# Merged weight words kept in SBUF, and a reordered passage from block 0 to block 1, in a convolution followed by an MLP

## The chip, the cores and the metric

One core of a Trainium2 chip runs the whole program. The metric is device time in microseconds (us), the median of several runs. One further execution was profiled; every row shown here comes from it. Engines: PE is TensorE, DVE VectorE, ACT ScalarE, POOL GpSimd, SP the queue that issues the DMAs.

## The reference

A convolution over the last 7 tokens whose weights differ by token and by head come out of a softmax, and then a two-layer MLP on 16384 tokens of width 192 with 2048 hidden units:

```python
w = softmax(weight_gen)                       # 7 taps, 8 heads
h_in = einsum('bshk,bskhg->bshg', w, windows_of(x_pad))
h = h_in.reshape(16384, 192) @ w_in           # 192 -> 2048
g = where(h >= 1, h, where(h <= -1, 0, (h + 1) ** 2 / 4))
out = g @ w_out                               # 2048 -> 192
```

## The kernel before

The 16384 tokens are 32 blocks of 512. For each block POOL makes the convolution (`conv`: seven products and six additions of 128x768 elements, L179 and L189). The result is turned (a transpose on DVE and a trip through DRAM from block 2 on, on PE for blocks 0 and 1) and split into a high part `hc` (ACT, L258) and a rest `hl` (L259; on DVE for blocks 0 and 1, on POOL from block 2 on).

The MLP runs over pairs: pair w is two slices of 128 hidden units; a block has NP = 8 pairs, so pair 8 is the first of block 1 and pair 16 the first of block 2. The first product of a pair, `gemm1_pair` (18 pairs of matmuls, L378), writes two of the four banks `ps_h` of PSUM. Then follow `relu` and `square` on ACT (L389, L392), `act_g` on DVE (L397), and `split_g`, which makes `gh` on ACT (L403) and `gl` on DVE (L404) and lets the pair's banks go. The second product, `gemm2_part` in two parts (L432), comes two pairs later on PE (LAGP = 2) and adds into the banks `o0` and `o1`; `evac` copies these out when a block is done. A matmul that takes a bank over to the other half of the rows waits for a note that passes over SP (L441).

During block 0 the weights are still being decoded, one chunk c for each pair: a cast (`cast_dve` L331, `cast_act` L327), then `merge` (L340, DVE) joins two halves of each word, `high` (L352, ACT) rounds the word to `whi` or `wo`, and `low` (L356, DVE) keeps the rest in `wlo` or `wo`. `merge` reads two tiles in SBUF (`r` and `head`) and writes `psw`, a tile from the four banks `ps_h`; `low` reads `psw` from PSUM and `whi` or `wo` from SBUF. `early_pair(w)` is the order of this work for pairs 2 to 6, with chunk w + 1; `first_pairs` is the same for the first chunks, `edge_pair` for pair 7, in which block 1 is turned (`turn1`) and split. The convolution of block 1 runs on POOL meanwhile; each of its steps waits for the last `merge` or cast ahead of it (`marks`, a dependency by hand).

All engines run in the order in which the code issues (a manual schedule). What belongs to later blocks is put into that order by a table, `at(w, place)`: the softmax of a group of two blocks (L149 to L155), the convolution, the turning and the splitting. For the group of blocks 3 and 4 (b == 3 in the table) the last softmax step, a multiplication, is POOL's; it stands between the convolutions of blocks 2 and 3 in POOL's order. The splitting of block 2 stands on POOL behind the first six steps of block 3's convolution.

Of the kernel before, what the change touches and what calls it, by code (L numbers as in the profile page):

```python
# [10 lines left out]
F32 = mybir.dt.float32  # L11
# [11 lines left out]
def kernel(  # L23
# [22 lines left out]
    P = 128  # L46
# [53 lines left out]
    def run(ops):  # L100
        for o in ops:
            o()
# [227 lines left out]
        o, i = tops(c, part)  # L330
        marks.append(nc.vector.tensor_scalar(out=o, in0=i, scalar1=0.5, scalar2=None, op0=ALU.mult))  # L331

    psw = {}

    def merge(c, part):
        word = raw_t[c].bitcast(U32)[:, 1:1 + 2 * CN].rearrange("p (c t) -> p c t", t=2)[:, :, 0]
        upper = heads[c % 2].rearrange("p c t -> p (c t)").bitcast(U32)
        psw[c, part] = ps_h.tile([P, 512], F32, tag="h", name="psw")
        sl = (slice(0, C1), slice(C1, CN))[part]
        marks.append(nc.vector.scalar_tensor_tensor(  # L340
            out=psw[c, part].bitcast(U32)[:, 0:sl.stop - sl.start], in0=word[:, sl], scalar=13, in1=upper[:, sl],
            op0=ALU.logical_shift_right, op1=ALU.bitwise_or))
# [48 lines left out]
    def square(i):  # L391
        nc.scalar.activation(out=u_t[i], in_=u_t[i], func=AF.Square, scale=UNIT ** -0.5)  # L392

    def act_g(i):

        uv, pv = u_t.pop(i), h_t[i][:, 0:N]
        nc.vector.scalar_tensor_tensor(out=pv, in0=uv, scalar=1.0 / UNIT, in1=pv, op0=ALU.min, op1=ALU.max)  # L397

    def split_g(i):
        gv = h_t.pop(i)[:, 0:N]  # L400
        gh = gp.tile([P, 512], F32R, tag="gh", name="gh")
        gl = gp.tile([P, 512], F32R, tag="gl", name="gl")
        nc.scalar.activation(out=gh[:, 0:N], in_=gv, func=AF.Copy)  # L403
        nc.vector.tensor_tensor(out=gl[:, 0:N], in0=gv, in1=gh[:, 0:N].bitcast(F32), op=ALU.subtract)  # L404
        g_t[i] = (gh, gl)
# [74 lines left out]
    def at(w, *ops, place=2):  # L480
        side.setdefault((w, place), []).extend(ops)
# [15 lines left out]
    for b in range(2, NB):  # L497
        w = (b - 2) * NP
        at(max(w - 5, 2), lambda b=b: clear_x(b))
        at({2: 4, 3: 8, 4: 14}.get(b, w - 3), lambda b=b: load_x(b), place=4 if b == 4 else 2)  # L500
        if b in first and b > 2:
            g = first[b]
            at({3: 5, 5: 12}.get(b, w - 9), lambda g=g: load_w(g))
            if b == 3:
                where = [(7, 4), (7, 4), (8, 4), (8, 4), (10, 4), (10, 4), (11, 2)]
            elif b == 5:
                where = [(18, 4), (19, 4), (20, 0), (20, 4), (21, 4), (22, 4), (23, 4)]
            else:
                where = [(w - 6 + k, 4) for k in range(7)]
            later(lambda g=g, b=b: softmax(g, nc.vector, nc.gpsimd if b == 3 else nc.vector), where)  # L510
        if b == 2:
            where = [(6, 2)] * 2 + [(7 + k // 3, 2) for k in range(2 * K - 3)]
        elif b == 3:
            where = [(v, 2) for v in (12, 12, 13, 13, 13, 13, 14, 14, 15, 15, 16, 16, 17)]
        elif b == 4:
            where = [(17 + k // 2, 2) for k in range(2 * K - 1)]
        else:
            where = [(w + CONV + k // 2, 2) for k in range(2 * K - 1)]
        later(lambda b=b: conv(b, nc.gpsimd), where)
        turned = [(w + TOUT, 2), (w + TOUT + 1, 0)] + [(w + TOUT + 2 + c, 0) for c in range(NC) for h in range(2)]  # L520
        where = [(w + SPLIT + k // 4, (0, 0, 4, 4)[k % 4]) for k in range(2 * NC)]
        if b == 2:
            turned = [(11, 0)] * 2 + [(12, 0)] * 2 + [(13, 0)] * 2 + [(14, 0)] * 2
            where = [(13, 4)] * 2 + [(14, 4)] * 2 + [(15, 0)] * 2
        elif b == 3:
            turned = [(w + 11, 0)] * 2 + [(w + 12, 0)] * 3 + [(w + 13, 0)] * 3
            where = [(w + 13, 4)] * 2 + [(w + 14, 0)] * 4
        elif b == 4:
            turned[0] = (w + TOUT, 4)
        later(lambda b=b: transpose_out(b), turned)  # L530
        later(lambda b=b: split_out(b, [nc.gpsimd] * NC), where)

    with tc.manual_schedule():
# [51 lines left out]
        def turn1(c):  # L585
            src1.append(ps_h.tile([P, 512], F32, tag="h", name="psx"))
            turn_sum(src1, turned1, True, True, c)
# [68 lines left out]
        def edge_pair(w):  # L656
            i, j = 2 * w, 2 * w + 1
            splits = split_x(1, src1, [nc.vector] * NC)
            relu(i)
            square(i)  # L660
            run(splits[0:1])
            act_g(i)
            run(splits[1:2])
            run(splits[2:3])
            run(splits[3:4])
            turn1(2)
            split_g(i)
            relu(j)
            run(splits[4:6])
            square(j)  # L670
            act_g(j)
            split_g(j)

        at(NP - 2, lambda: again(turned1), place=4)
        at(NP - 1, lambda: turn1(0), lambda: turn1(1), place=5)
        for w in range(NS // 2 + LAGP):
            i, j = 2 * w, 2 * w + 1
            copies, store = [], None
            if i < NS and w != 1:
                gemm1_pair(w)  # L680
            run(side.pop((w, 5), []))
            if w >= LAGP:
                gemm2_part(w - LAGP, 0)
                if w == NP - 1:
                    edge_pair(w)
                gemm2_part(w - LAGP, 1)
                pb, pf = steps[j - 2 * LAGP]
                if pf == NF - 1:
                    copies, store = evac(pb)
                    if i < NS:  # L690
                        at(w + (5 if pb else 6), store, place=0)
            if w < NP:
                run(side.pop((w, 0), []))
                if w == 0:
                    first_pairs()
                elif 1 < w < NP - 1:
                    early_pair(w)
                run(side.pop((w, 2), []))
            else:
                if i < NS:  # L700
                    relu(i)
                    square(i)
                run(side.pop((w, 0), []))
                if i < NS:
                    relu(j)
                if i < NS:
                    square(j)
                    act_g(i)
                    act_g(j)
                if i < NS:  # L710
                    run(copies)
                else:
                    for m in range(n // 2 if store else 0):
                        run(copies[2 * m:2 * m + 2])
                        store(m)
                run(side.pop((w, 2), []))
                if i < NS:
                    split_g(i)
                    split_g(j)
            run(side.pop((w, 4), []))  # L720
# [31 lines left out]
```

## Time and profile before

| | us |
|---|---|
| median of 3 runs | 1144.56 (1143.82 to 1144.73) |
| profiled execution | 1144.88 |
| its span, first to last instruction | 1142.4 |
| PE busy | 1128.4 (99%) |
| ACT busy | 964.5 (84%) |
| DVE busy | 834.3 (73%) |
| POOL busy | 792.4 (69%) |

The span is cut short by 2.5 us against the execution's own time. The shares are means over stages that differ: nearly all of PE's idle time lies in the first 60 us, so the stages have to be read one by one.

### The profile page before, as it was taken

How to read it: one execution, taken by the hardware profiler on the slowest of the kernel's cores; microseconds unless marked ns; L12 is line 12 of the kernel's file. 1: busy time of each engine (PE TensorE's matmuls, PEld its weight loads, DVE VectorE, ACT ScalarE, POOL GpSimd, SP SyncE). 2: the span in 40 equal slices, each digit the busy share in tenths (PEclk: the TensorE clock that was granted, in tenths of full speed). 3: DMA queues.
4: the chain of work that ended last, by engine and by line, in shares of the span. 5: the costliest groups of instructions: out<-in, count | busy, mean ns of one | idle time of the engine just before them, and what ended most of it. 6: DMA issues, size and time to landing. Idle time of an engine off the chain costs nothing.

```text
span 1142.4 us, 32241 instructions
## 1 busy us (share of the span) xinstructions
PE 1128.4 (99%) x12885; PEld 1112.8 (97%) x12885; DVE 834.3 (73%) x1271; ACT 964.5 (84%) x1745; POOL 792.4 (69%) x511
## 2 busy tenths in 40 slices
PE   7999999999999999999999999999999999999998
PEld 5889999999999999999999999999999999999998
DVE  8887867777676777767777677776767777677765
ACT  6878888888888888888888888888888888888886
POOL 4699876777857678486686866778576785866310
PEclk9899999999999999999999999999999999999999
DMA  9512222222222122222122222222222122221100
GB/s 230 116 67 83 92 85 92 72 64 79 90 78 91 59 74 89 73 96 90 44 90 73 86 91 78 65 73 90 77 92 72 61 91 82 81 91 43 48 24 29
DMA packets 84053, 91.43 MB, mean 80 GB/s; under 512 B 5056, under 2 KB 75712, under 8 KB 83904
## 3 DMA queue, kind: packets, MB, share of 16 engines
q1 hardware_dynamic: 83904, 89.39, 24.6%
q8 instruction: 101, 1.65, 0.6%
q14 instruction: 48, 0.39, 0.1%
HBM read 64.99 MB, written 24.38 MB: 78 GB/s over the span
## 4 chain that ended last, share of the span: by engine, by line
PE 96%; ACT 1%; DVE 1%; DMA 0%; POOL 0%; issue 0%; SPq 0%; DVEq 0%; POOLq 0%
PE psh L378 49%; PE o L432 46%; PE psx L267 1%; DMA x<-in_x_dram 0%; ACT u L392 0%; ACT u L389 0%; ACT gh L403 0%; DVE psh L397 0%; DVE psw L340 0%; ACT whi L352 0%; POOL piece L189 0%; POOL acc L189 0%; ACT wo L352 0%; DVE gl L404 0%; DVE wo L356 0%
## 5 line engine op out<-in xcount | busy, mean ns | idle before, releaser
L432 PE MATMUL o<-wo,gh 64*128 64x384 f32 x4096 | 638.3, 353 | 1.0 <-SPq L441 1.0
L432 PE MATMUL o<-wo,gl 64*128 64x192 f32 x4096 | 615.1, 247 | 0.0
L432 PEld LDWEIGHTS o<-wo,gh 64*128 64x128 f32 x4096 | 609.3, 184 | 2.4 <-SPq L441 1.2
L432 PEld LDWEIGHTS o<-wo,gl 64*128 64x128 f32 x4096 | 591.3, 188 | 0.7
L397 DVE SCALAR_TENSOR_TENSOR psh<-u,psh 128x512 f32<-128x512 f32 x512 | 354.4, 695 | 282.2 <-ACT u L392 281.8
L378 PE MATMUL psh<-hc,whi 64*128 64x512 f32 x1536 | 436.6, 396 | 3.6 <-DVE wlo L356 2.5
L378 PE MATMUL psh<-hc,wlo 64*128 64x512 f32 x1536 | 430.5, 389 | 0.0
L378 PE MATMUL psh<-hl,whi 64*128 64x512 f32 x1536 | 429.5, 388 | 0.0
L389 ACT ACTIVATE u<-psh 128x512 f32<-128x512 f32 x512 | 301.4, 589 | 79.0 <-PE psh L378 77.8
L404 DVE TENSOR_TENSOR gl<-psh,gh 128x512 fp32r<-128x512 f32 x512 | 345.2, 684 | 15.5 <-ACT gh L403 1.1
L403 ACT ACTIVATE gh<-psh 128x512 fp32r<-128x512 f32 x512 | 299.0, 591 | 64.7 <-DVE psh L397 64.7
L189 POOL TENSOR_TENSOR acc<-acc,pr 128x768 f32<-128x768 f32 x185 | 343.4, 1856 | 6.5 <-DVE head L331 2.8
L392 ACT ACTIVATE u<-u 128x512 f32<-128x512 f32 x512 | 324.3, 633 | 16.0
L179 POOL TENSOR_TENSOR pr<-x,w 128x768 f32<-128x768 f32 x186 | 286.6, 1548 | 7.0 <-DVE psw L340 7.0
L378 PEld LDWEIGHTS psh<-hc,whi 64*128 64x128 f32 x1536 | 270.6, 185 | 8.7 <-DVE wlo L356 3.9
L378 PEld LDWEIGHTS psh<-hl,whi 64*128 64x128 f32 x1536 | 270.5, 185 | 3.1 <-DVE hl L259 0.3
L378 PEld LDWEIGHTS psh<-hc,wlo 64*128 64x128 f32 x1536 | 270.9, 186 | 1.6
L259 POOL TENSOR_TENSOR hl<-XT,hc 128x512 fp32r<-128x512 f32 x90 | 115.8, 1303 | 206.9 <-PE o L432 151.6
L179 POOL TENSOR_TENSOR acc<-x,w 128x768 f32<-128x768 f32 x31 | 47.9, 1546 | 70.2 <-DVE w L155 68.3
L258 ACT ACTIVATE hc<-XT 128x512 fp32r<-128x512 f32 x90 | 55.5, 618 | 0.0
L284 DVE STREAM_TRANSPOSE T<-acc 128x768 f32<-128x768 f32 x30 | 50.2, 1672 | 0.0
L457 DVE SCALAR_TENSOR_TENSOR osb<-o,osb 128x384 f32<-128x384 f32 x64 | 32.5, 548 | 2.8 <-ACT osb L456 2.8
(44 smaller groups left out, 188.8 us busy)
## 6 DMA issues: line engine op xcount, KB each, us to landing
x<-in_x_dram SPq DMA_DIRECT2D x28, 960.0 KB, 5.0
XT<-D SPq DMA_DIRECT2D x180, 128.0 KB, 2.7
out_dram<-osb SPq DMA_DIRECT2D x31, 384.0 KB, 3.1
D<-T SPq DMA_DIRECT2D x30, 384.0 KB, 2.3
x<-in_x_dram SPq DMA_DIRECT2D x4, 945.0 KB
w<-in_weight_gen_dram SPq DMA_DIRECT2D x15, 224.0 KB, 2.6
r<-in_moe_w_in_dram SPq DMA_DIRECT2D x16, 192.0 KB, 7.3
r<-in_moe_w_out_dram SPq DMA_DIRECT2D x8, 384.0 KB, 12.5
```

Source lines behind the costliest of these rows:

```text
L179: held(eng.tensor_tensor(out=t, in0=xtile[:, k:k + n, :].rearrange("p j (h g) -> p j h g", h=H), in1=wt[:, gi, :, :, k:k + 1].to_broadcast ...
L189: held(eng.tensor_tensor(out=o, in0=s, in1=t, op=ALU.add))
L258: ops.append(lambda c=c: nc.scalar.activation(out=hc[:, c], in_=src[c], func=AF.Copy))
L259: ops.append(lambda c=c: lows.append(engines[c].tensor_tensor(out=hl[:, c], in0=src[c], in1=hc[:, c].bitcast(F32), op=ALU.subtract)))
L284: lambda: nc.vector.transpose(out=T.rearrange("p b c j -> p b j c"), in_=acc.rearrange("p j (r b) -> p b j r", b=R)),
L378: nc.tensor.matmul(out=pair[h][:, 0:N], lhsT=l[rows, f // 2, (c + h) % NC if b < 2 else c], rhs=r[rows, c], start=(s == 0), stop=(s == len ...
L389: nc.scalar.activation(out=u_t[i], in_=h_t[i][:, 0:N], func=AF.Relu, scale=0.5 * UNIT, bias=0.5)
L392: nc.scalar.activation(out=u_t[i], in_=u_t[i], func=AF.Square, scale=UNIT ** -0.5)
L397: nc.vector.scalar_tensor_tensor(out=pv, in0=uv, scalar=1.0 / UNIT, in1=pv, op0=ALU.min, op1=ALU.max)
L403: nc.scalar.activation(out=gh[:, 0:N], in_=gv, func=AF.Copy)
L404: nc.vector.tensor_tensor(out=gl[:, 0:N], in0=gv, in1=gh[:, 0:N].bitcast(F32), op=ALU.subtract)
L432: mm = nc.tensor.matmul(out=o_t[b][turn][:, k, 0:cols], lhsT=g_t[i][l][rows, t * P:(t + 1) * P], rhs=wo[rows, f].rearrange("p s d -> p (s ...
```

## The change

Three edits, and one table row. First, `merge` writes a tile `words` in SBUF, of which one is made for the whole run, with four slots (two chunks, two parts), in the one buffer that the turned blocks (`XT`) use later. The four `ps_h` banks are left to the first product and to block 1's turning. Second, the second product of pair 6 is issued within `edge_pair(7)`, in front of block 1's first product, and the first two turns of block 1 come after the first part of pair 5's second product. Third, the copies of block 0's result come before the squares of pair 9, and the third split of block 1 comes after a square. The softmax table of the group of blocks 3 and 4 moves by one to two pairs.

```diff
-    psw = {}
+    psw, words = {}, []
...
-        psw[c, part] = ps_h.tile([P, 512], F32, tag="h", name="psw")
+        if not words:
+            words.append(xt.tile([P, 4, C1], F32, tag="XT", name="words", bufs=1))
+        psw[c, part] = words[0][:, 2 * part + c % 2]
...
             if b == 3:
-                where = [(7, 4), (7, 4), (8, 4), (8, 4), (10, 4), (10, 4), (11, 2)]
+                where = [(9, 4), (9, 4), (10, 0), (10, 4), (11, 4), (11, 4), (12, 0)]
...
             run(splits[2:3])
             run(splits[3:4])
+            gemm2_part(w - LAGP, 1)
+            gemm2_part(w - 1, 0)
             turn1(2)
+            gemm2_part(w - 1, 1)
             split_g(i)
             relu(j)
-            run(splits[4:6])
             square(j)
             act_g(j)
+            run(splits[4:6])
             split_g(j)
 
         at(NP - 2, lambda: again(turned1), place=4)
-        at(NP - 1, lambda: turn1(0), lambda: turn1(1), place=5)
...
-            run(side.pop((w, 5), []))
             if w >= LAGP:
-                gemm2_part(w - LAGP, 0)
+                if w != NP:
+                    gemm2_part(w - LAGP, 0)
                 if w == NP - 1:
+                    turn1(0)
+                    turn1(1)
                     edge_pair(w)
-                gemm2_part(w - LAGP, 1)
+                elif w != NP:
+                    gemm2_part(w - LAGP, 1)
...
                     relu(i)
+                    if w == NP + 1:
+                        run(copies)
+                        copies = []
                     square(i)
```

DVE in an early pair of block 0, from the merges of one chunk on. Before:

```order
L340 SCALAR_TENSOR_TENSOR psw<-r,head 128x384 x2
L356 TENSOR_TENSOR wlo<-psw,whi 128x384
L356 TENSOR_TENSOR wo<-psw,wo 128x2x192
L397 SCALAR_TENSOR_TENSOR psh<-u,psh 128x512
L331 TENSOR_SCALAR head<-r 128x384
```

And after:

```order
L342 SCALAR_TENSOR_TENSOR words<-r,head 128x384 x2
L358 TENSOR_TENSOR wlo<-words,whi 128x384
L358 TENSOR_TENSOR wo<-words,wo 128x2x192
L399 SCALAR_TENSOR_TENSOR psh<-u,psh 128x512
L331 TENSOR_SCALAR head<-r 128x384
```

The order is the same; the word that `low` reads is now a tile in SBUF, as `whi` and `wo` are.

DVE in pairs 10 and 11 (block 1): the ends of the softmax of blocks 3 and 4 (`s`) and the transpose of block 2 (`T`). Before:

```order
L397 SCALAR_TENSOR_TENSOR psh<-u,psh 128x512 x2
L404 TENSOR_TENSOR gl<-psh,gh 128x512 x2
L153 TENSOR_SCALAR s<-s 128x64
L154 RECIPROCAL s<-s 128x64
L284 STREAM_TRANSPOSE T<-acc 128x6x4x32
L397 SCALAR_TENSOR_TENSOR psh<-u,psh 128x512 x2
L404 TENSOR_TENSOR gl<-psh,gh 128x512 x2
```

And after:

```order
L399 SCALAR_TENSOR_TENSOR psh<-u,psh 128x512 x2
L406 TENSOR_TENSOR gl<-psh,gh 128x512 x2
L152 TENSOR_REDUCE s<-w 128x64
L284 STREAM_TRANSPOSE T<-acc 128x6x4x32
L399 SCALAR_TENSOR_TENSOR psh<-u,psh 128x512 x2
L406 TENSOR_TENSOR gl<-psh,gh 128x512 x2
L153 TENSOR_SCALAR s<-s 128x64
L154 RECIPROCAL s<-s 128x64
```

The reciprocal, for which POOL's multiplication waits, has moved behind pair 11's work and behind the transpose. POOL's own order is the same in both kernels.

PE from the third turn of block 1 to the products that follow it (a second product is 16 such rows of L432, of which the last or first stand here). Before:

```order
L267 MATMUL psx<-ident,piece 128x128 x4
...
L432 MATMUL o_408<-wo,gl 128x192 x2
L378 MATMUL psh<-hc,whi 128x512 x2
...
L378 MATMUL psh<-hl,whi 128x512 x2
L432 MATMUL o_407<-wo,gh 128x384 x2
```

And after:

```order
L267 MATMUL psx<-ident,piece 128x128 x4
...
L434 MATMUL o_403<-wo,gl 128x192 x2
L380 MATMUL psh<-hc,whi 128x512 x2
...
L380 MATMUL psh<-hl,whi 128x512 x2
L380 MATMUL psh<-hc,whi 128x512 x2
```

Before, pair 6's second product stood between the first products of pairs 8 and 9; now these two follow each other.

## Rows read from the trace of the kernel before

**Rows 1.** Windows: busy PE, PEld, DVE, ACT, POOL (us), granted clock, DMA.

```profile
30.00:40.00 10.00, 9.84 (x72) 8.69 (x74) 8.77 (x18) 7.97 (x16) 6.31 (x4) 0.67 0.92 182
60.00:80.00 20.00, 20.00 (x230) 18.18 (x230) 16.66 (x25) 14.67 (x27) 19.07 (x12) 1.00 0.16 52
```

**Rows 2.** Timeline of DVE, one early pair: start, duration, line, operation.

```profile
44.89 1.02 DVE L340 SCALAR_TENSOR_TENSOR psw<-r,head 128x384 uint32<-128x384 uint32 x2
46.01 0.56 DVE L356 TENSOR_TENSOR wlo<-psw,whi 128x384 fp32r<-128x384 f32 x1
46.48 0.55 DVE L356 TENSOR_TENSOR wo<-psw,wo 128x384 fp32r<-128x384 f32 x1
...
50.11 1.02 DVE L340 SCALAR_TENSOR_TENSOR psw<-r,head 128x384 uint32<-128x384 uint32 x2
```

**Rows 3.** Timeline of POOL: block 1's convolution in block 0.

```profile
19.11 0.98 POOL L155 TENSOR_TENSOR w<-w,s 128x448 f32<-128x448 f32 x1 [7.11 <-DVE psw L340]
21.92 1.54 POOL L179 TENSOR_TENSOR acc<-x,w 128x768 f32<-128x768 f32 x1 [1.83 <-DVE psw L340]
23.42 3.05 POOL L179 TENSOR_TENSOR pr<-x,w 128x768 f32<-128x768 f32 x2
...
46.06 1.55 POOL L179 TENSOR_TENSOR pr<-x,w 128x768 f32<-128x768 f32 x1 [1.33 <-DVE psw L340]
...
53.19 1.85 POOL L189 TENSOR_TENSOR piece<-acc,pr 128x768 f32<-128x768 f32 x1
```

**Rows 4.** Timeline, POOL: a product during block 1.

```profile
114.20 1.56 POOL L179 TENSOR_TENSOR pr<-x,w 128x768 f32<-128x768 f32 x1
```

**Rows 5.** Timeline, DVE: one subtraction twice, both inputs in SBUF.

```profile
114.56 1.68 DVE L150 TENSOR_TENSOR w<-w,m 128x448 f32<-128x448 f32 x1
...
183.48 0.61 DVE L150 TENSOR_TENSOR w<-w,m 128x448 f32<-128x448 f32 x1
```

**Rows 6.** Groups by line and shape: count, busy us, mean ns.

```profile
L356 DVE TENSOR_TENSOR wlo<-psw,whi 128x384 fp32r<-128x384 f32 x8 | 4.4, 547 | 1.4 <-ACT whi L352 1.2
```

**Rows 7.** The same view for ACT, split from SBUF and from PSUM.

```profile
L258 ACT ACTIVATE hc<-XT 128x512 fp32r<-128x512 f32 x90 | 55.5, 618 | 0.0
...
L258 ACT ACTIVATE hc<-psx 128x512 fp32r<-128x512 f32 x6 | 3.2, 594 | 0.4 <-PE psx L267 0.3
```

**Rows 8.** Timeline of DVE, first chunks.

```profile
19.55 1.02 DVE L356 TENSOR_TENSOR wo<-psw,wo 128x384 fp32r<-128x384 f32 x2
...
22.30 0.54 DVE L356 TENSOR_TENSOR wlo<-psw,whi 128x384 fp32r<-128x384 f32 x1
...
28.42 1.03 DVE L340 SCALAR_TENSOR_TENSOR psw<-r,head 128x384 uint32<-128x384 uint32 x2
```

**Rows 9.** Timeline of PE: where pair 8's first product begins.

```profile
59.82 0.42 PE L378 MATMUL psh<-hc,whi 64*128 64x512 f32 x2
```

**Rows 10.** The chain that ended last: one second product, start and us.

```profile
62.05 2.25 PE o L432 x32
```

**Rows 11.** Timeline of DVE, pairs 10 and 11.

```profile
73.79 1.45 DVE L404 TENSOR_TENSOR gl<-psh,gh 128x512 fp32r<-128x512 f32 x2
75.16 1.80 DVE L153 TENSOR_SCALAR s<-s 128x64 f32<-128x64 f32 x1
...
77.46 1.61 DVE L284 STREAM_TRANSPOSE T<-acc 128x768 f32<-128x768 f32 x1
...
80.33 1.29 DVE L404 TENSOR_TENSOR gl<-psh,gh 128x512 fp32r<-128x512 f32 x2
```

**Rows 12.** Timeline of PE: first product of pair 13; then, pair 16's end.

```profile
81.45 0.72 PE L378 MATMUL psh<-hc,whi 64*128 64x512 f32 x2
...
96.37 0.39 PE L378 MATMUL psh<-hl,whi 64*128 64x512 f32 x1
```

**Rows 13.** Timeline of POOL: softmax's multiplication, splits of block 2.

```profile
77.68 0.98 POOL L155 TENSOR_TENSOR w<-w,s 128x448 f32<-128x448 f32 x1 [0.78 <-ACT u L392]
...
93.36 2.71 POOL L259 TENSOR_TENSOR hl<-XT,hc 128x512 fp32r<-128x512 f32 x2
```

## Prediction

> **What bounds the kernel now.** I read the windows first. From 60 us on PE has no idle time [rows 1], so work taken off another engine there gives nothing, and a stop that the change puts into PE's row there costs its whole length. Block 0, before that, is another matter. I read it on DVE's timeline: the merges of one chunk begin at 44.89 and those of the next at 50.11, 5.22 us apart [rows 2], while PE needs 2 x 2.25 at most for a pair (a second product is 2.25 [rows 10], a first product no more). So in block 0 DVE paces the pairs, and PE waits for it. [...] The third thing to see is how POOL and DVE meet. At 114.56 a DVE subtraction with both inputs in SBUF takes 1.68 us where the same one takes 0.61 at 183.48, with POOL idle [rows 5]. POOL's product of that time ends at 114.20 + 1.56 = 115.76 [rows 4]; the subtraction ends at 116.24, so it began to run at 115.63, about 0.13 before the product's recorded end. It waited for nearly the whole of POOL's instruction. `low` at 46.48 takes 0.55 in the midst of POOL's product of 46.06 [rows 2, 3]: with the word in PSUM it has one input in SBUF, and does not wait.
>
> **Words in SBUF.** `low` gets two inputs in SBUF (16 times); `merge` had them already, and POOL's steps wait for it by hand. The instructions themselves do not change in price: `low` takes 547 ns for 384 elements from PSUM [rows 6], the subtraction 0.61 for 448 from SBUF [rows 5], about the same per element. [...] ACT's `high` reads SBUF too: 618 against 594 ns for a split [rows 7], 16 x 0.02 = 0.4 us, taken as nothing because ACT waits for DVE in these pairs; without that cover it is 0.4.
>
> The wait is the cost. In an early pair POOL's product starts 1.17 us after the first merge, and the first `low` 1.12 after it [rows 2, 3]. Whichever is first, one `low` waits for a product: if POOL, the first `low`; if DVE, POOL waits half a microsecond and then holds off the second. That is 1.55 - 0.13 = 1.42 on DVE. It swallows the waits for ACT that DVE has now, such as the 0.1 between 44.89 + 1.02 and 46.01 [rows 2], which I put at 0.2 for a pair: 5.22 becomes 6.4. If the second `low` could run on ahead of a waiting POOL, that case would cost nothing; no row shows two such DVE instructions in a row against POOL, so the bounds are 0 and 1.42. I take 1.42, since the row at 114.56 shows that who waits gets the port at the next instruction's end. [...]
>
> From the merges of chunk 3 (28.42 [rows 8]) to those of chunk 7 (50.11) four periods took 21.7; they become 4 x 6.4 = 25.6: +3.9. Ahead of them lie the first chunks. The pair of `low` at 19.55 [rows 8] waits for POOL's softmax step of 19.11 (0.98 [rows 3]), which now starts behind the `low` in front of it: about 0.75. The `low` at 22.30 comes some 0.4 behind the start of POOL's first product (21.92): 1.55 - 0.13 - 0.4 = 1.0. The next meets POOL's second product, queued right behind (23.42): 1.42. Together 3.2. So chunk 7's merges come 7.1 late. POOL's last two additions wait for these merges and then for one `low` (0.5): the convolution of block 1, which ended at 53.19 + 1.85 = 55.04 [rows 3], ends 7.6 late.
>
> **Pair 6's second product.** Pair 8's first product started at 59.82 [rows 9], 4.8 after that end. Now 2.25 of pair 6 stand in front of it, and the first part of pair 5's second product (1.1) runs while PE waits for POOL. So it starts at 59.82 + 7.6 + 2.25 - 1.1 = 68.6. Of this 2.25 is work taken from behind, so the end moves by 68.6 - 59.82 - 2.25 = **+6.5**.
>
> The move has a price behind it. Pairs 8 and 9 now follow each other on PE, so from there PE stands 2.25 nearer to ACT and DVE than before. The first product of pair w + 2 takes the banks that `gl` of pair w lets go. Pair 10's `gl` ended at 73.79 + 1.45 = 75.24 and pair 11's at 80.33 + 1.29 = 81.62 [rows 11]; pair 13's first product began at 81.45 [rows 12], with no slack; pair 12's, one period earlier ((81.45 - 59.82) / 5 = 4.33), at 77.12, with 1.9. Less 2.25 these are -2.2 and -0.4. For pair 11 the table gives back some: between the two `gl` stood `s`, reciprocal and transpose (75.16 to about 79); now only a reduction, taken like the subtraction's 0.61, and the transpose, 1.61, stand there: about 1.6 less. For pair 10 it takes: the maximum and the subtraction (0.6 each) now come right ahead of it, and the subtraction meets POOL, busy 19.07 of 20 us [rows 1]: up to 1.4 more. That the copies come sooner only shifts 1 us from one pair to the next. The stops add up to between 1 and 2.5; I take **+2.0**, nearer the upper end because POOL is almost never idle there.
>
> **Softmax later.** In POOL's order the multiplication stands in front of block 3's convolution, and that in front of block 2's splits. It started at 77.68, having waited 0.78 for the reciprocal [rows 13]. From the end of pair 10's `gl` (75.24) the reciprocal now comes behind a reduction 0.6, the transpose 1.6, pair 11's four instructions (twice about the 1.4 of two `gl`) and its own two steps (0.7, without POOL in the way): at 80.9 at the earliest, so the multiplication starts 3.3 later, and with PE 0.25 nearer (2.25 less the 2.0 of stops) 3.5. The last split of block 2 ended at 93.36 + 2.71 = 96.07 [rows 13]; PE reads it at 96.37 [rows 12]. The slack is 0.3, and what pair 10's delay adds is about as much: PE stops for **+3.5** in pair 16's first product (2.8 to 4.2). The steps of POOL's queue in between cannot be passed. SP's queue is not disturbed: no DMA changes its place, and the shared buffer costs nothing, since block 2's first writes into it follow the transpose of 77.46 [rows 11], long after the last `low`.
>
> **Clock.** In block 0 a low clock is covered, because PE has 6.4 us for a pair. The stop of 3.5 us in pair 16 is longer than any ahead of the fall at 30 us, so I expect one more fall, worth 0 to 3.3 [rows 1]; I take half, **+1.6**.
>
> Sum: 6.5 + 2.0 + 3.5 + 1.6 = 13.6 on the profiled execution's 1144.88 (span 1142.4 and 2.5 around it); the median of the runs is 0.3 lower, 1158.2. I lower it by 0.7 for waits in the first chunks that the delay swallows: **1157.5**.
>
> **Rivals.** (a) The second `low` gets ahead of POOL where DVE is first: only the first chunks pay, 0.75 + 1.0, with POOL's 0.5, less the 1.1: about +1; with the 7.1 of the other terms 1152.7. For it: 1.12 against 1.17 us. (b) `low` does not meet POOL at all: then +6.5 becomes -1.1 to -1.6, and the sum +5.5: 1150. Against it: rows 4 and 5. (c) The other side: as (b), and PE gains what the freed banks allow. With nothing held by `psw`, PE begins each pair before the `low` is done, its clock does not fall at 30 us (-3.3), and block 1's start fills up (-1.6); with the +2.0 that is -2.9: 1141.7. The point that decides is the multiplication on POOL: if it starts no more than 0.3 us later relative to pair 16, PE does not stop there. Against it stands that the reciprocal is issued one pair later. (d) PE's clock stays low through most of block 0, so that PE, not DVE, paces there: a pair of 4.3 us takes up to 8.6 instead of 6.4; two such pairs give 4.4 more: 1162.
>
> **How the numbers follow.** Chances: forecast 50%, (a) 18%, (b) 15%, (c) 7%, (d) 10%. The range reaches from (b) with no fall of the clock (1148.5) to (d)'s beginning (1161.5); it leaves out (c), half of (d) and the lowest of (b). A measurement of this kernel tells apart about 0.2%, 2.3 us. Faster by more than that is half of (c) and a little: 0.05; within it the rest of (c) and the low end of (b): 0.06; slower 0.89.
>
> **What would show it.** On DVE, `low` rows of 1.9 to 2.0 us beside POOL's products, and merges 6.4 apart; pair 8's first product near 68; PE stops for `gl` near pairs 12 and 13; on POOL an idle time of 4 to 5 us in front of the multiplication, and on PE a stop of about 3.5 us in pair 16, waiting for POOL's `hl`. It is wrong if `low` keeps 0.55 beside POOL's products, or if POOL's splits of block 2 end before PE needs them.

## The result

The changed kernel takes 1156.66 us (median of 5 runs, 1156.2 to 1157.78) against 1144.56 for the kernel before (5 runs, 1143.82 to 1148.27): a ratio of 1.0104, 95% interval 1.0088 to 1.012. The forecast was 1157.5, slower. The profiled execution took 1156.72, its span is 1154.9, 12.5 longer than before.

### Where the 12.5 us arise

The first product of pair w begins, in the timeline of PE, so much later than before (us, from the traces; a minus is earlier):

| pair | changed kernel | what lies in between |
|---|---|---|
| 8 | +7.66 | block 0, and pair 6's second product (2.25) in front |
| 10 | +5.41 | block 0 alone |
| 14 | +6.89 | pairs 10 to 13: +1.48 |
| 17 | +12.43 | pair 16: +5.54 |
| 30 and all later | +12.61 | nothing more |

So all of it arises in the first 111 us, at three places.

**Block 0.** The windows of the changed kernel for the stretches of [rows 1], with the 5 us ahead of them, and then those around pair 16 (us; busy time of PE, PEld, DVE, ACT and POOL; granted clock; DMA share; GB/s):

```profile
25.00:30.00 5.00, 4.81 (x38) 3.77 (x36) 4.87 (x7) 2.92 (x6) 2.77 (x2) 0.66 1.10 200
30.00:40.00 10.00, 7.06 (x72) 5.52 (x72) 9.67 (x16) 7.96 (x17) 4.88 (x3) 1.00 0.94 185
60.00:80.00 20.00, 19.00 (x209) 16.74 (x207) 14.61 (x25) 14.85 (x29) 20.00 (x13) 1.00 0.15 50
...
105.00:110.00 5.00, 3.87 (x30) 3.36 (x32) 0.73 (x2) 2.32 (x5) 5.00 (x4) 0.77 0.01 3
110.00:115.00 5.00, 5.00 (x56) 4.66 (x54) 2.12 (x4) 2.52 (x6) 4.92 (x4) 0.89 0.00 0
```

From 30 to 40 us DVE is busy for 9.67 of 10 us with 16 instructions, where it was 8.77 with 18. That PE has fallen from 9.84 to 7.06 is the clock: it ran 72 matmuls in both, at 1.00 now and at 0.67 before. In the changed kernel the clock falls sooner, to 0.66 from 25 to 30 us. From 40 to 60 us, with the clock at 1.00 in both, DVE is busy for 19.40 instead of 17.04 us and PE for 15.79 instead of 18.84: there PE waits, and DVE paces it. The idle 1.00 us of PE from 60 to 80 us is one wait, of 0.96 at 62.13, ahead of block 1's turning. Two early pairs on DVE (timeline: start, duration, line, operation), to be laid beside [rows 2]:

```profile
37.36 1.02 DVE L342 SCALAR_TENSOR_TENSOR words<-r,head 128x384 uint32<-128x384 uint32 x2
38.51 0.56 DVE L358 TENSOR_TENSOR wlo<-words,whi 128x384 fp32r<-128x384 f32 x1
38.98 1.91 DVE L358 TENSOR_TENSOR wo<-words,wo 128x384 fp32r<-128x384 f32 x1
...
41.41 0.38 DVE L331 TENSOR_SCALAR head<-r 128x384 f16<-128x384 bf16 x1
...
43.65 1.01 DVE L342 SCALAR_TENSOR_TENSOR words<-r,head 128x384 uint32<-128x384 uint32 x2
```

And POOL beside them, with the last step of block 1's convolution, which answers to the end of [rows 3]:

```profile
38.52 1.95 POOL L179 TENSOR_TENSOR pr<-x,w 128x768 f32<-128x768 f32 x1 [1.03 <-DVE words L342]
...
59.69 2.03 POOL L189 TENSOR_TENSOR piece<-acc,pr 128x768 f32<-128x768 f32 x1
```

POOL's product is issued at 38.52, 0.01 behind the first `low`, and takes 1.95 instead of the 1.55 of [rows 3]: it waits for that `low`. The second `low` is issued at 38.98 and takes 1.91 instead of 0.55, ending at 40.89: it waits for the product, which ends at 40.47. The merges stand 6.29 apart (37.36, 43.65) instead of 5.22. The convolution ends at 61.72 instead of 55.04.

**Pairs 10 to 13** cost 1.48. One `gl` makes PE wait there, for 0.27; the other 1.2 us are in no wait that PE's list shows:

```profile
83.84 0.49 PE L380 MATMUL psh<-hc,whi 64*128 64x512 f32 x1 [0.27 <-DVE gl L406]
```

**Pair 16.** POOL's row, and PE's stop (timelines; in brackets the idle time ahead and what ended it), answering to [rows 13] and [rows 12], and ahead of POOL's row the reciprocal on DVE, before and after:

```profile
76.99 0.55 DVE L154 RECIPROCAL s<-s 128x64 f32<-128x64 f32 x1
...
88.64 0.55 DVE L154 RECIPROCAL s<-s 128x64 f32<-128x64 f32 x1
```

```profile
89.33 0.98 POOL L155 TENSOR_TENSOR w<-w,s 128x448 f32<-128x448 f32 x1 [5.76 <-ACT u L394]
...
104.52 2.52 POOL L259 TENSOR_TENSOR hl<-XT,hc 128x512 fp32r<-128x512 f32 x2
```

```profile
105.85 0.50 PE L380 MATMUL psh<-hl,whi 64*128 64x512 f32 x2 [2.88 <-POOL hl L259]
...
107.09 0.50 PE L380 MATMUL psh<-hl,whi 64*128 64x512 f32 x2 [0.28 <-POOL hl L259]
```

The bracket names ACT's `u`, but in both kernels the multiplication starts 0.14 behind the end of the reciprocal (77.54 and 89.19). It waits for 5.76 instead of 0.78 and starts 4.8 later than before by the clock of pair 16 (89.33 - 77.68 - 6.89). The last two splits, queued behind it and eight convolution steps, end at 107.04, and PE stops twice, for 3.2 in all. Then the granted clock falls: 0.77 and 0.89 in the two windows above, so 0.23 x 5 + 0.11 x 5 = 1.7 us. The other 0.7 of the 5.54 I put to matmuls that run less closely one behind the other around the stop (0.50 for an entry at full clock, where [rows 12] has 0.39). They are there without a fall of the clock too: with the words back in PSUM (below) the clock is 1.00 from 100 to 110 us, PE stops in pair 16 for 1.69 and 0.28, and the pair loses 2.7.

### The profile page after: what moved, and what is told of

Read it like the earlier page. It is cut to its first block, busy times and chain, and to the rows that moved or that the text cites. A ratio compares the mean times of both kernels' runs of the same rounds, so it can differ in the third digit from the quotient of the medians.

```text
span 1154.9 us, 32233 instructions
## 1 busy us (share of the span) xinstructions
PE 1132.1 (98%) x12885; PEld 1112.2 (96%) x12885; DVE 842.5 (73%) x1271; ACT 965.6 (84%) x1745; POOL 794.6 (69%) x511
## 4 chain that ended last, share of the span: by engine, by line
PE 93%; DVE 3%; ACT 2%; issue 1%; POOL 1%; DMA 0%; SPq 0%; DVEq 0%; POOLq 0%
PE psh L380 46%; PE o L434 46%; DVE psh L399 1%; DVE wo L358 1%; PE psx L267 1%; ACT gh L405 1%; PE psx L208 0%; DVE wlo L358 0%; DVE gl L406 0%; ACT u L394 0%; DVE words L342 0%; ACT whi L354 0%; ACT u L391 0%; DMA XT<-D 0%; POOL hl L259 0%
## 5 line engine op out<-in xcount | busy, mean ns | idle before, releaser
L434 PE MATMUL o<-wo,gh 64*128 64x384 f32 x4096 | 625.4, 354 | 0.2 <-DVE gl L406 0.2
L434 PE MATMUL o<-wo,gl 64*128 64x192 f32 x4096 | 599.5, 248 | 0.0
L434 PEld LDWEIGHTS o<-wo,gh 64*128 64x128 f32 x4096 | 579.7, 185 | 1.9 <-DVE gl L406 0.9
L434 PEld LDWEIGHTS o<-wo,gl 64*128 64x128 f32 x4096 | 575.3, 188 | 0.6
L380 PE MATMUL psh<-hc,whi 64*128 64x512 f32 x1536 | 392.2, 396 | 7.7 <-ACT whi L354 7.3
L380 PE MATMUL psh<-hc,wlo 64*128 64x512 f32 x1536 | 386.8, 390 | 3.6 <-DVE wlo L358 3.2
L380 PE MATMUL psh<-hl,whi 64*128 64x512 f32 x1536 | 385.4, 388 | 3.2 <-POOL hl L259 3.2
L380 PEld LDWEIGHTS psh<-hc,whi 64*128 64x128 f32 x1536 | 227.8, 184 | 12.7 <-ACT whi L354 9.3
L380 PEld LDWEIGHTS psh<-hc,wlo 64*128 64x128 f32 x1536 | 228.3, 185 | 7.7 <-DVE wlo L358 5.7
L380 PEld LDWEIGHTS psh<-hl,whi 64*128 64x128 f32 x1536 | 227.5, 184 | 7.1 <-POOL hl L259 4.0
## 6 DMA issues: line engine op xcount, KB each, us to landing
r<-in_moe_w_out_dram SPq DMA_DIRECT2D x8, 384.0 KB, 12.5
```

Source lines behind the costliest of these rows:

```text
L380: nc.tensor.matmul(out=pair[h][:, 0:N], lhsT=l[rows, f // 2, (c + h) % NC if b < 2 else c], rhs=r[rows, c], start=(s == 0), stop=(s == len ...
L434: mm = nc.tensor.matmul(out=o_t[b][turn][:, k, 0:cols], lhsT=g_t[i][l][rows, t * P:(t + 1) * P], rhs=wo[rows, f].rearrange("p s d -> p (s ...
```

## The experiments

All times of this section are medians; the kernel before had 1143.55 to 1143.7 in these sessions. For each run the table shows how much later than before the first products of four pairs begin (us, from the traces):

| run | time | ratio, 95% interval | pair 7 | pair 10 | pair 14 | pair 17 |
|---|---|---|---|---|---|---|
| changed kernel | 1156.66 | 1.0088 to 1.012 | +5.5 | +5.4 | +6.9 | +12.4 |
| words back in PSUM | 1150.21 | 1.0041 to 1.0071 | +0.1 | -1.0 | +3.3 | +6.0 |
| only words in SBUF | 1151.26 | 1.0048 to 1.0082 | +5.6 | +6.8 | +6.7 | +6.7 |
| old softmax table | 1150.56 | 1.0047 to 1.0077 | +5.5 | +5.4 | +6.6 | +6.6 |
| only new softmax table | 1150.26 | 1.0049 to 1.0079 | -0.3 | -0.3 | -0.2 | +6.0 |
| only PE's order and the copies | 1143.62 | 0.9989 to 1.0007 | -0.9 | -2.0 | -0.9 | -0.8 |
| POOL held back | 1154.96 | 1.0073 to 1.0104 | +2.2 | +2.2 | +5.9 | +11.1 |
| POOL held back, cast first | 1153.17 | 1.0064 to 1.0094 | +2.5 | +2.5 | +6.2 | +11.3 |
| splits first | 1152.97 | 1.0061 to 1.0092 | +3.3 | +3.2 | +6.4 | +6.5 |
| new softmax, splits first | 1145.57 | 1.0006 to 1.0024 | -1.1 | -1.1 | +0.9 | +1.0 |
| the same, subtraction on POOL | 1143.62 | 0.9992 to 1.0009 | -1.3 | -1.3 | -1.2 | -1.1 |
| changed kernel, mended | 1144.37 | 0.9995 to 1.0013 | -1.0 | -2.1 | -0.5 | -0.5 |

Differences below about 1 us in a column can be those of single executions. The columns rest on one trace of the kernel before, of an execution that took 1144.88, 1.2 to 1.3 above its medians here; a kernel that is as fast as that one usually is can therefore stand at -1.

### Taking the change apart

**Words back in PSUM**, in the changed kernel:

```diff
-        if not words:
-            words.append(xt.tile([P, 4, C1], F32, tag="XT", name="words", bufs=1))
-        psw[c, part] = words[0][:, 2 * part + c % 2]
+        psw[c, part] = ps_h.tile([P, 512], F32, tag="h", name="psw")
```

> The changed kernel with the merged words back in PSUM; the order of pair 6's second product, the copies and the softmax table stay changed. Port theory: `low` has one input in SBUF again and takes 0.55 us beside POOL's products, so block 0 is as before and the moved product gains 1.1 to 1.6 (pair 9's first product about 1.5 early against before). The losses behind it stay: 1.5 for banks in block 1, 5.5 in pair 16 (stop for POOL's split and low clock). Sum about +5.5: 1150. Rival, the loss of block 0 comes from the order of PE's work and not from the words: 1156 to 1157, pair 9 still 5.4 late.

**Only words in SBUF**: the same edit the other way, in the kernel before.

> The kernel before with one edit, the merged words in SBUF. Port theory: one `low` of every chunk waits for a POOL step, the convolution of block 1 ends 6.7 late as in the changed kernel (61.7 against 55.0), and with nothing else moved PE, DVE and POOL are late by the same, so pair 16 does not stop: +6.5 to 7, 1151 to 1152. Rival, the freed banks help by themselves: 1142 to 1144.

Measured 1150.21 and 1151.26. Block 0 goes as expected: with PSUM words pair 10 starts 1.0 sooner than before, with SBUF words alone 6.8 later. The words cost 6.4 to 6.8 us there, and PE's order gives 1.0 to 1.4 of it back. But the first total agrees with its expectation in part by luck: of the 6.4 us gained in block 0, 2.9 are lost again by pair 14 (+4.3 instead of +1.5), and pair 16's stop is 2.8 shorter (+2.7 instead of +5.5). In block 1, PE stops for `gl` in pair 12 for 1.47 and 0.27, and the clock falls behind that (0.66 from 80 to 85 us, worth 1.7). Why `gl` is so late is settled below.

**Old softmax table**, in the changed kernel, and **only new softmax table**, in the kernel before:

```diff
-                where = [(9, 4), (9, 4), (10, 0), (10, 4), (11, 4), (11, 4), (12, 0)]
+                where = [(7, 4), (7, 4), (8, 4), (8, 4), (10, 4), (10, 4), (11, 2)]
```

> The changed kernel with the softmax table of before. If the later reciprocal makes pair 16 stop, POOL's multiplication follows the convolution of block 2 by under 1 us again instead of 5.8, pair 16 does not wait for POOL's split, and no low clock follows: 5 less than the changed kernel, 1151 to 1152. Rival, PE stops there because it stands 2.25 us nearer to POOL since pair 6's product moved: the stop stays at 2 us or more, 1154 to 1157.

> The kernel before with one edit, the softmax table of the changed kernel. Multiplication about 3.3 later, slack at pair 16 of 0.3 and 0.4 of idle on POOL ahead of the splits: PE stops for 2.6, and with a low clock behind it up to 4.3: 1147.2 to 1148.9. Rival, the stop needs the moved product too: 1144 to 1145.

Measured 1150.56 and 1150.26. With the old table pair 16 does not stop (+6.65 at pair 16 and +6.64 at pair 17); with the new one alone it stops and nothing else happens. The second run missed its numbers: 6.7 us instead of 2.6 to 4.3. Its trace, POOL first, then PE:

```profile
82.26 0.98 POOL L155 TENSOR_TENSOR w<-w,s 128x448 f32<-128x448 f32 x1 [5.68 <-ACT u L392]
...
97.46 2.49 POOL L259 TENSOR_TENSOR hl<-XT,hc 128x512 fp32r<-128x512 f32 x2
```

```profile
98.77 0.79 PE L378 MATMUL psh<-hl,whi 64*128 64x512 f32 x2 [2.89 <-POOL hl L259]
```

and its windows:

```profile
95.00:100.00 5.00, 2.11 (x13) 1.24 (x10) 1.98 (x3) 1.93 (x4) 5.00 (x5) 0.80 0.36 148
100.00:105.00 5.00, 5.00 (x38) 4.90 (x38) 2.30 (x4) 3.43 (x6) 5.00 (x4) 0.52 0.02 5
105.00:110.00 5.00, 5.00 (x60) 4.52 (x58) 1.48 (x3) 2.79 (x6) 4.92 (x4) 1.00 0.00 0
```

The stop is about the expected one, 2.9 for 2.6. What was mis-sized is what follows it: 0.80 from 95 to 100 and 0.52 from 100 to 105 are 0.20 x 5 + 0.48 x 5 = 3.4 us of clock (0.50 on the mean from 98 to 103 us), twice the fall of the changed kernel, and a little of it lies within the stop itself. So this stop of 2.9 cost 6.2 (-0.2 at pair 16, +6.0 at pair 17).

### What the later softmax waits for

**Splits first**, in the changed kernel: of the eight steps of block 3's convolution in front of the last split of block 2, three go behind it.

```diff
-            where = [(v, 2) for v in (12, 12, 13, 13, 13, 13, 14, 14, 15, 15, 16, 16, 17)]
+            where = [(v, 2) for v in (12, 12, 13, 13, 14, 15, 15, 15, 15, 16, 16, 16, 17)]
```

> The changed kernel with block 2's three splits earlier in POOL's row: of the eight convolution steps of block 3 that stood ahead of the last split, three now stand behind it; nothing else moves. If pair 16 stops because the splits stand behind the steps that the later softmax delays, the last split ends near 102 instead of 107, the stop of 2.9 and 0.3 us and the fall of the clock behind it go, and the time is 5.0 to 5.6 lower: 1151 to 1151.7. Rival: the splits then wait for the gathers or for ACT's high parts, and a part of the stop stays: 1153 to 1156.

**New softmax, splits first**: the same row and the new softmax table in the kernel before.

> The kernel before with the softmax of block 3 two pairs later, as in the run that did this alone, and with block 2's splits ahead of three of block 3's convolution steps in POOL's row. If all that the later softmax costs is the stop in pair 16, it goes, and the time is that of the kernel before less the 0.2 to 0.3 by which pairs 8 to 16 began sooner in that run: 1143 to 1143.7. Rival: the later softmax has a price of its own beside POOL's row (DVE's subtraction and reciprocal beside `gl`): 1145 to 1147.

In both the stop of pair 16 is gone (pair 17 stands where pair 16 stood, within 0.1), so POOL's order made it. Neither total is what was expected: 1152.97 in the one (four runs, two near 1151 and two at 1154.6; the traced one, 1151.38, is where it was expected) and 1145.57 in the other, 1.9 over the kernel before. In both, pairs 10 to 13 lose more than in the changed kernel: 3.3 and 2.0 us. Here is DVE in the second of these runs, and POOL beside it:

```profile
70.49 0.61 DVE L149 TENSOR_REDUCE m<-w 128x64 f32<-128x448 f32 x1
71.21 2.76 DVE L150 TENSOR_TENSOR w<-w,m 128x448 f32<-128x448 f32 x1
```

```profile
70.12 1.56 POOL L179 TENSOR_TENSOR pr<-x,w 128x768 f32<-128x768 f32 x1
71.63 1.85 POOL L189 TENSOR_TENSOR acc<-acc,pr 128x768 f32<-128x768 f32 x1
```

The softmax's subtraction takes 2.76 us instead of the 0.61 of [rows 5]; it waits to the end of a product of POOL's and through the whole of the addition behind it. Every `gl` behind it is nearly 2 us late, and PE stops for it in pair 12 (0.92, in the row here, and 0.27 us):

```profile
77.11 0.49 PE L378 MATMUL psh<-hc,whi 64*128 64x512 f32 x1 [0.92 <-DVE gl L404]
```

It is the same in four more runs: 2.39 with PSUM words, 2.58 in the changed kernel with splits first, 2.97 and 2.99 in the two runs with POOL held back that follow below, and PE's first wait for `gl` in pair 12 is 1.47, 1.64, 2.06 and 2.07 there. In the changed kernel itself the subtraction happens to come 0.26 before a step of POOL's ends and takes 0.75:

```profile
79.19 0.75 DVE L150 TENSOR_TENSOR w<-w,m 128x448 f32<-128x448 f32 x1
```

The splits change nothing in the order up to pair 12, so two pairs of runs have the same order up to there and differ in this subtraction. With the new table the subtraction took 0.95 without the splits first and pairs 10 to 13 lost 0.2; with them it took 2.76, and they lost 2.0. In the changed kernel it took 0.75 and 1.48 were lost, with the splits first 2.58 and 3.3.

**The same, subtraction on POOL**, and the maximum one pair sooner:

```diff
-                where = [(9, 4), (9, 4), (10, 0), (10, 4), (11, 4), (11, 4), (12, 0)]
+                where = [(8, 4), (8, 4), (10, 0), (10, 4), (11, 4), (11, 4), (12, 0)]
...
-            later(lambda g=g, b=b: softmax(g, nc.vector, nc.gpsimd if b == 3 else nc.vector), where)
+            later(lambda g=g, b=b: softmax(g, *[nc.gpsimd if b == 3 else nc.vector] * 2), where)
```

> The kernel before with the later softmax and block 2's splits first, as in the run that did these two, and with the maximum one pair sooner and the subtraction on POOL. There pairs 10 to 14 lost 2.1 us beside a subtraction of 2.76 on DVE. If that subtraction is the cause, the loss goes, and the time is 1142.6 to 1143.7. Rival, as for the kernel with the move: 1145 to 1146.

Measured 1143.62. The loss in pairs 10 to 13 goes from 2.0 to 0.1. On POOL the subtraction costs 1.00, in a row that waits later anyway:

```profile
66.62 1.00 POOL L150 TENSOR_TENSOR w<-w,m 128x448 f32<-128x448 f32 x1
```

This run moves the maximum as well, and the two were not run apart; with the pairs of runs above, the subtraction is what fits. So the price that is left of the later softmax was DVE's subtraction waiting for POOL. With splits and subtraction mended it costs nothing, and it gains nothing that can be measured.

### What PE's order is worth

**Only PE's order and the copies**: the changed kernel with PSUM words and the old softmax table.

> The changed kernel with its words back in PSUM and the softmax of block 3 at its old places: what is left is pair 6's second product in front of block 1's first, the copies of block 0 sooner and block 1's split in its new order. If the move's gain and its price are as the runs so far put them (pair 9 starts 1.0 sooner with PSUM words in the changed order; between pairs 9 and 14 the changed kernel with the old softmax loses 1.2), it comes out at the kernel before: 1143 to 1144.5. In the run with words in PSUM and the late softmax, pairs 9 to 14 lost 4.3, with a fall of the clock; if that belongs to the PE order and not to the softmax's place, this run gives 1146 to 1148. Rival: the move is a pure gain of 1 us, 1142.5.

**The changed kernel, mended**: PSUM words, splits first, subtraction on POOL.

> The changed kernel with words in PSUM, with block 2's splits ahead of three convolution steps of block 3, and with the maximum of block 3's softmax one pair sooner and its subtraction on POOL instead of DVE (there, POOL is idle for 5 to 8 us ahead of the multiplication). If what the later softmax costs in block 1 is DVE's subtraction waiting for a step of POOL's (2.4 to 2.8 us where it takes 0.6 to 0.75 without), the stop of about 1.5 us and the fall of the clock in pair 12 go, and the move's gain of 1 to 2 us stays: 1141.5 to 1143.5. Rival: `gl` is late there for other DVE work (the sum, the transpose, the reciprocal), and pairs 10 to 14 still lose 3 to 4: 1145 to 1147.

Measured 1143.62 and 1144.37, neither to be told from the kernel before (both intervals contain 1; the second median is 0.8 higher). With pair 6's second product in front, pair 10 starts 2.0 to 2.1 sooner than before (0.9 to 1.0 of that is already there at pair 7, before the move acts), and pairs 10 to 13 give back 1.1 to 1.6, in pieces too small to stand in PE's list of waits. The move gains about 1 us where PE used to wait for POOL and returns it in block 1. That it does so because PE, now nearer to DVE, waits for it is argued and not shown; the runs with the old PE order and a subtraction of under 1 us, only words in SBUF and only the new table, lose 0.2 or less in these pairs. The rival of a pure gain fell; the second run's 1141.5 to 1143.5 was too low by about 1 us for the same reason. That the first run loses 1.1 there, and the one with PSUM words and the new softmax 4.4, shows that most of the latter belonged to the softmax's place: 1.7 of stops and 1.7 of clock.

### What the words in SBUF wait for

**POOL held back**: in the changed kernel the steps of block 1's convolution wait for the two `low` of their chunk as well.

```diff
-        nc.vector.tensor_tensor(out=lo, in0=src, in1=hi.bitcast(F32), op=ALU.subtract)
+        marks.append(nc.vector.tensor_tensor(out=lo, in0=src, in1=hi.bitcast(F32), op=ALU.subtract))
...
             high(c, 0)
             high(c, 1)
-            wave(1)
             low(c, 0)
             low(c, 1)
+            wave(1)
             square(i)
```

(`wave(1)` issues one step of POOL's; the first chunks are treated alike.)

> The changed kernel, words in SBUF, but POOL's steps of block 1's convolution in block 0 wait for the two subtractions `low` of their chunk and not only for its merges, so that no `low` is queued behind a step of POOL's. If the shared port is what the words in SBUF cost, the `low` rows of block 0 go back to about 0.55 us, merges of two chunks stand 5.2 to 5.5 us apart, the convolution of block 1 ends near 56, and the time falls by some 5 us to 1150 to 1152 (the 1.2 to 1.5 of block 1 and the 5.5 of pair 16 stay). Rival: the words in SBUF are slow for another reason (the write of the merge, ACT's read): merges stay 6.3 apart and the time is 1156 to 1157, or above it because POOL now starts later.

Here are the groups of DVE's rows from 28 to 58 us by line and shape (count, busy us, mean ns, idle time ahead), in the changed kernel:

```profile
L358 DVE TENSOR_TENSOR wo<-words,wo 128x384 fp32r<-128x384 f32 x5 | 8.5, 1691 | 0.0
...
L358 DVE TENSOR_TENSOR wlo<-words,whi 128x384 fp32r<-128x384 f32 x5 | 4.1, 830 | 0.6
...
L331 DVE TENSOR_SCALAR head<-r 128x384 f16<-128x384 bf16 x5 | 1.9, 378 | 0.0
```

and with POOL held back:

```profile
L331 DVE TENSOR_SCALAR head<-r 128x384 f16<-128x384 bf16 x5 | 5.8, 1160 | 0.0
...
L358 DVE TENSOR_TENSOR wlo<-words,whi 128x384 fp32r<-128x384 f32 x5 | 2.8, 558 | 0.6
L358 DVE TENSOR_TENSOR wo<-words,wo 128x384 fp32r<-128x384 f32 x5 | 2.8, 553 | 0.0
```

The two `low` are back at 558 and 553 ns, the times with the word in PSUM [rows 2, 6]. So nothing but POOL made them slow; the rival falls. But the time is 1154.96, not 1150 to 1152. Block 0 gains 3.2 us, and block 1, with the subtraction at 2.97, takes 2.2 of it back. In block 0 now the cast behind them, which has a single input, waits for POOL's product (1160 instead of 378 ns), and merges stand 5.97 apart.

**POOL held back, cast first**: in addition the cast of the next chunk is issued in front of the two `low`.

```diff
             merge(c, 0)
             merge(c, 1)
+            if c + 1 < NCH:
+                cast_dve(c + 1, 1)
...
-            if c + 1 < NCH:
-                cast_dve(c + 1, 1)
             wave(1)
```

> The run with POOL's steps held back until both `low` of a chunk are through, and with DVE's 16-bit cast of the next chunk (the `head` row) issued ahead of the two `low` instead of behind them, so that it too is queued behind no step of POOL's. In the run before this one the `low` rows were back at 0.55 us but the cast took 1.3 to 1.4 instead of 0.38, and the merges of two chunks stood 5.97 apart. If what paces block 0 is the time that DVE's instructions with all operands in SBUF and POOL's two steps take one after the other (1.02 + 0.38 + 1.02 + 1.55 + 1.85 = 5.8 us for a pair), moving the cast only moves the wait, on to the next merges: 5.8 to 6.0 apart, and the time 1153 to 1155, as in that run. Rival: the cast was all that was left of the cost; then the merges go to 5.2 to 5.4 apart and the time to 1150 to 1152.

Measured 1153.17 (the traced execution is the longest of four, 1156.26; the others took 1151.89 to 1153.24). The merges stand 5.59 apart, and the wait has moved on to them:

```profile
41.60 1.36 DVE L342 SCALAR_TENSOR_TENSOR words<-r,head 128x384 uint32<-128x384 uint32 x2
42.88 0.38 DVE L331 TENSOR_SCALAR head<-r 128x384 f16<-128x384 bf16 x1
...
47.19 1.35 DVE L342 SCALAR_TENSOR_TENSOR words<-r,head 128x384 uint32<-128x384 uint32 x2
```

Merges that take 1.36 instead of 1.02 while `low` and cast are at their own times are what the sum predicts, not the rival. The 5.59 itself lies between the two forecasts, 5.8 to 6.0 and 5.2 to 5.4, and the times of the four runs reach into both ranges of time, so it is the rows that decide. The sum's 5.8 was 0.2 too long. If the end of each of POOL's steps is recorded 0.13 late, as the prediction read at 114.56, the sum is 5.8 - 2 x 0.13 = 5.56, near the 5.59. So with words in SBUF an early pair has 2.4 us of DVE's work and 3.4 of POOL's that exclude each other, and by this sum no order of them brings it below about 5.6, an estimate that one order bears out; with words in PSUM only 1.4 us of DVE's do, and DVE's own 5.2 us pace the pair. In both runs block 0 is still 2.2 to 2.5 late at pair 10, and block 1 takes back more, as told above.

## Why the prediction was right

**Words in SBUF: right, 1 us too dear.** It gave 7.6 for the convolution's end and, less 1.1 for PE's order, +6.5. Measured are 6.68 for the end (61.72 against 55.04), 6.8 at pair 10 for the words alone, 1.0 to 1.4 for PE's order, and 5.41 together. The mechanism is as described: whoever is first, one `low` is 1.35 to 1.37 us longer beside a product of POOL's (1.42 was forecast); at 32.21 POOL was first, by 0.04, and the first `low` took 1.92. That `low` by itself costs the same from SBUF held as well: 553 to 558 ns with POOL held back, against 547 [rows 6]. The period was 6.28 (6.4). Four of them make 25.1 from chunk 3's merges (31.07) to those of chunk 7 (56.21), where 25.6 was forecast. The first chunks made 2.65 (31.07 - 28.42), with 3.2 forecast. So both parts were too dear by half a microsecond, and the 0.7 that the prediction took off at the end was owed here.

**Rival (a) fell by the row at 38.98.** DVE is first by 0.01 us at 38.51, POOL's product then waits and is through before the second `low`. So the step that was chosen without a row, 1.42 and not 0, was right. In these rows the one that is issued second waits for the other, on either engine: 1.95 for 1.55 on POOL and then 1.91 for 0.55 on DVE. What the prediction and the expectations call the port is a name for this waiting; the rows show the waiting and no port. **Rival (b)** is what POOL held back tried by hand, and even that gave 1154.96.

**Pair 8's first product** was forecast at 68.6 and came at 67.48, by the same 1 us.

**Block 1: +2.0 forecast, +1.48 measured, for a reason that could have come out otherwise.** That the move costs something there was right: with the old softmax table it cost 1.2, with PE's order alone 1.1. The stops for `gl` that were to make up the term are hardly seen, 0.27 of it. And its largest item, the subtraction that meets POOL ("up to 1.4 more"), did not occur in the changed kernel, where it took 0.75. In five runs with other timing it took 2.39 to 2.99, and pairs 10 to 13 cost 3.3 to 4.4 in the four of them that have the changed order of PE. The term's bounds were too narrow: up to 2.5 was allowed. That the forecast came so near in total is here in part luck.

**Softmax later: +3.5 and +1.6 forecast, 5.54 measured.** The place, the engine and the wait were right: an idle time of 5.76 in front of the multiplication (4 to 5 forecast), a stop of 2.9 and 0.3 (3.5) in pair 16 for `hl`, and one more fall of the clock, 1.7 (1.6). The delay of 4.8, where 3.5 was forecast, was mis-sized at pair 10: its `gl` ended 1.7 later by the clock of pair 16 (82.34 + 1.45, against 75.24, less 6.89), where the prediction allowed for about 0.5. The stop was smaller than that delay, because POOL's row from there to the end of the splits took 17.7 instead of 18.4 and the splits had some slack. That the fall came out near the half that was taken is luck: in the run with the new table alone the same stop made a fall of twice that (3.4 us), for which no run here shows the cause.

**The clock in block 0** was said to be covered by DVE's pace. In the run with the new softmax table alone the clock never fell there (1.00 from 25 to 40 us, against 0.67 in [rows 1]), and pair 7 came only 0.3 sooner. That agrees, and it takes away the ground of rival (c), which counted 3.3 us for it (0.33 x 10, [rows 1]). Rival (d) counted with half the clock, 8.6 us for 4.3, through most of block 0; the trace of before shows the half from 30 to 35 us:

```profile
30.00:35.00 5.00, 4.84 (x23) 3.91 (x25) 4.43 (x9) 3.77 (x8) 3.10 (x3) 0.50 1.10 224
```

It fell with the changed kernel's windows: the clock was low from 25 to 30 us (0.66) and 1.00 from 30 to 60, not low through most of block 0.

**Sum.** 5.41 + 1.48 + 5.54 = 12.43, with 13.6 - 0.7 = 12.9 forecast on the same execution. The first two terms were too high by 1.1 and 0.5, of which the 0.7 taken off covers a part, and the third was too low by 0.4: the total is a little nearer than its parts.

## What to carry to other kernels

Before a tile is moved from PSUM to SBUF to free a bank, list every DVE instruction that reads it and ask whether it then has both inputs in SBUF, and add its time to POOL's in that stage: here 1.0 us of subtractions for each pair became exclusive with 3.4 of POOL's, and the pair's period grew from 5.2 to 6.3, to 5.6 in the best order tried. A step that is issued later in a table delays everything queued behind it on its engine, in this case splits of another block that had 0.3 us of slack; moving it back cures that, and so does putting the urgent rows in front. And a stop in a row that PE paces is to be counted with the clock that may fall behind it: 3.2 us cost 5.5, 2.9 cost 6.2, and 2.0 without a fall cost 2.7. In these runs the clock fell behind both stops of about 2.9 us whose windows stand above, to 0.77 and to 0.52, and from pair 14 to 17 the two runs with POOL held back lost about as much as these, 5.2 and 5.1; of six stops of 0.9 to 2.1 us in pairs 12 and 16 it fell behind one, of 1.47 (0.66 from 80 to 85 us), and not behind one of 2.06 (1.00 from 80 to 90 us, POOL held back), so a price without the clock and one with it belong in the range.

## What the runs showed of the hardware that I had not expected

- A DVE cast with one input, from SBUF to SBUF in 16 bits, waits for POOL like an instruction with two inputs: 1.30 to 1.38 us in four rows beside POOL's products (POOL held back; 1160 ns on the mean of five), 378 ns without (the changed kernel); I had not counted it. The softmax's reduction does not wait: 0.61 at 70.49 in the kernel with new softmax and splits first, in the middle of POOL's product of 70.12.
- A waiting DVE instruction does not always get in at the end of the step that it waits for. At 114.56 in the trace of before it did [rows 4, 5], and at 79.19 in the changed kernel too; over all traces the subtraction (128x448, beside a step of POOL's) got in so in 18 rows. In six rows, of five other runs, POOL's next step, queued right behind, went first, and the subtraction waited for that one as well (2.37 to 2.99 us). What decides between the two I could not find. The time by which DVE was there ahead of the step's end does not decide it (0.2 to 1.8 us where it got in, 0.1 to 0.7 where it was passed over): with the new table alone it was there 0.48 ahead and got in, with the splits first as well 0.47 ahead and was passed over.
- Whether the two `low` of chunk 2 met POOL's first products depended on when a DMA landed. In the changed kernel with splits first that product waited for `x` until 23.82 and both `low` at 22.63 were through at 0.54 each; with the words alone it started at 22.62 and they took 1.91 and 1.90. That is the 2.2 us by which pair 10 differs between that run and the changed kernel, though nothing was changed ahead of pair 10. It may also be why that run's times lie in two groups 3.5 us apart; only one of the four runs was traced, so this is not shown.
